# Linear attention and a gated feed-forward in one kernel: groups of 256 tokens in quadrants of the array, with loads and weights gated in order

## The chip, the cores and the metric

One Trainium2 chip, one core of it. The metric is the device time of one execution in microseconds (us), the median over several runs. The profile takes one execution apart; its span is 1.7 to 1.8 us shorter than the time of the same run. PE is the tensor engine, PEld its weight loads, DVE the vector engine (VectorE), ACT the scalar engine (ScalarE), POOL is GpSimd, SP the engine that issues transfers. A run counts as slow when it is over 1.5% above the fastest of the same kernel.

## The reference

Lightning attention (linear attention with a decay per head) and a gated feed-forward on its result, everything in float32:

```python
# q, k, v: [4, 8, 768, 64] (batch, head, token, dim); lam: [8], 0.97 to 0.99
for b in range(nb):                                     # blocks of 64 tokens
    qb, kb, vb = ...
    intra = np.einsum('bhic,bhjc->bhij', qb, kb) * Dmask[None]      # causal lam**(i-j)
    intra = np.einsum('bhij,bhjd->bhid', intra, vb)
    inter = np.einsum('bhid,bhde->bhie', qb * lam_pow[None], kv_state)
    out[:, :, sl] = intra + inter
    kv_state = lam_block * kv_state + np.einsum('bhsd,bhse->bhde', kb * rev_pow, vb)
...
x = out.transpose(0, 2, 1, 3).reshape(3072, 512)
g = x @ w_gate                                          # [512, 1536]
return (g / (1 + np.exp(-g)) * (x @ w_val)) @ w_out     # [1536, 512]
```

Both kernels work in blocks of 128 tokens, which gives the same result.

## The kernel before

Attention goes by pairs of heads: two heads of 64 dimensions fill the 128 rows of the array, q and k are transposed on PE against an identity, and a block of 128 tokens of two pairs is one round, of scores, masks, state reads, products with v and a state update:

```python
for h2 in range(2):                                     # 24 such transfers for one batch
    nc.gpsimd.dma_start(out=q_nat[:, :, h2, :], in_=q_5d[b, hp, h2])   # 96 KB, casts to bf16
    nc.gpsimd.dma_start(out=k_nat[:, :, h2, :], in_=k_5d[b, hp, h2])
    nc.sync.dma_start(out=v_raw[:, :, h2, :], in_=v_5d[b, hp, h2])
...
nc.gpsimd.dma_start(out=wg_sb, in_=moe_w_gate...)       # all gate weights at once, then
nc.gpsimd.dma_start(out=wv_sb, in_=moe_w_val...)        # all value weights, then batch 1
...
nc.tensor.matmul(sp[:, 0, cs], st["kT"][0:64, bs], st["qT"][0:64, bs], start=True, stop=True)
nc.tensor.matmul(sp[:, 1, cs], st["kT"][64:128, bs], st["qT"][64:128, bs], start=True, stop=True)
... # (two halves of the array's rows at a time)
nc.vector.scalar_tensor_tensor(out=st["kv"], in0=st["kv"], scalar=lamblk[hp],
                               in1=up[:, ci, :], op0=ALU.mult, op1=ALU.add)
```

The feed-forward goes by tiles of 512 tokens and by chunks of 128 of the 1536 hidden columns: four gate and four value matmuls of 512 columns per chunk, twelve out matmuls per 128 tokens. Rounds of attention are spread between its chunks.

Of the kernel before, what the change touches and what calls it, by code (L numbers as in the profile page):

```python
# [8 lines left out]
FP32 = mybir.dt.float32  # L10
# [11 lines left out]
def kernel(  # L22
# [11 lines left out]
    nc = tc.nc  # L34

    B, H, S, D = q.shape
# [5 lines left out]
    NTOK = B * S  # L42
    MCHUNKS = DM // 128
    FCHUNKS = DFF // 128
    TT = 512
    NTT = NTOK // TT
    TSUB = 128
    CW = 2
# [3 lines left out]
    xtpool = ctx.enter_context(tc.tile_pool(name="xtpool", bufs=1))  # L52

    qkt_pool = ctx.enter_context(tc.tile_pool(name="qkt", bufs=8))
    nat_pool = ctx.enter_context(tc.tile_pool(name="nat", bufs=8))
    raw_pool = ctx.enter_context(tc.tile_pool(name="raw", bufs=6))
    kv_pool = ctx.enter_context(tc.tile_pool(name="kv", bufs=8))
    ssb_pool = ctx.enter_context(tc.tile_pool(name="ssb", bufs=6))

    hsb_pool = ctx.enter_context(tc.tile_pool(name="hsb", bufs=2))  # L60
    silu_pool = ctx.enter_context(tc.tile_pool(name="silu", bufs=3))
    osb_pool = ctx.enter_context(tc.tile_pool(name="osb", bufs=3))

    apool = ctx.enter_context(tc.tile_pool(name="apool", bufs=3, space=bass.MemoryType.PSUM))
    s_psum = ctx.enter_context(tc.tile_pool(name="s_psum", bufs=1, space=bass.MemoryType.PSUM))
    gate_pool = ctx.enter_context(tc.tile_pool(name="gate_pool", bufs=2, space=bass.MemoryType.PSUM))
    val_pool = ctx.enter_context(tc.tile_pool(name="val_pool", bufs=1, space=bass.MemoryType.PSUM))

    identity = const.tile([128, 128], BF16)
    make_identity(nc, identity)  # L70

    causal01 = const.tile([128, 128], BF16)
    make_upper_triangular(nc, causal01, val=1.0, diag=True)

    iota_free_p1 = const.tile([128, 128], FP32)
    nc.gpsimd.iota(iota_free_p1, pattern=[[1, 128]], base=1, channel_multiplier=0,
                   allow_small_or_imprecise_dtypes=True)
    iota_rev = const.tile([128, 1], FP32)
    nc.gpsimd.iota(iota_rev, pattern=[[0, 1]], base=BLK - 1, channel_multiplier=-1,
                   allow_small_or_imprecise_dtypes=True)  # L80

    lam_bcast = const.tile([128, H], FP32)
    nc.gpsimd.dma_start(out=lam_bcast,
                        in_=bass.AP(tensor=lam.tensor, offset=lam.offset, ap=[[0, 128], [1, H]]))

    q_5d = q.rearrange("b (hp h2) (blk p) d -> b hp h2 p blk d", h2=2, p=128)
    k_5d = k.rearrange("b (hp h2) (blk p) d -> b hp h2 p blk d", h2=2, p=128)
    v_5d = v.rearrange("b (hp h2) (blk p) d -> b hp h2 p blk d", h2=2, p=128)

    loaded = {}  # L90

    def attn_load(b, hp):
        def run():
            q_nat = raw_pool.tile([128, NBLK, 2, D], BF16, name="q_nat", tag="q_nat")
            k_nat = nat_pool.tile([128, NBLK, 2, D], BF16, name="k_nat", tag="k_nat")
            v_raw = nat_pool.tile([128, NBLK, 2, D], FP32, name="v_raw", tag="v_raw", bufs=5)
            for h2 in range(2):
                nc.gpsimd.dma_start(out=q_nat[:, :, h2, :], in_=q_5d[b, hp, h2])  # L98
                nc.gpsimd.dma_start(out=k_nat[:, :, h2, :], in_=k_5d[b, hp, h2])  # L99
                nc.sync.dma_start(out=v_raw[:, :, h2, :], in_=v_5d[b, hp, h2])  # L100
            loaded[(b, hp)] = dict(q_nat=q_nat, k_nat=k_nat, v_raw=v_raw)
        return run

    for hp in range(HP):
        attn_load(0, hp)()

    wg_sb = wpool.tile([128, MCHUNKS, DFF], BF16)
    wv_sb = wpool.tile([128, MCHUNKS, DFF], BF16)
    wo_sb = wpool.tile([128, FCHUNKS, DM], BF16)
    nc.gpsimd.dma_start(out=wg_sb, in_=moe_w_gate.rearrange("(c p) f -> p c f", p=128))  # L110
    nc.gpsimd.dma_start(out=wv_sb, in_=moe_w_val.rearrange("(c p) f -> p c f", p=128))
    for hp in range(HP):
        attn_load(1, hp)()
    nc.gpsimd.dma_start(out=wo_sb, in_=moe_w_out.rearrange("(c p) m -> p c m", p=128))

    ln_lam = const.tile([128, H], FP32)
    nc.scalar.activation(ln_lam, lam_bcast, AF.Ln)

    qscale = []
    revmat = []  # L120
    lamblk = []
    maskp_all = const.tile([128, 2, HP, 128], BF16)
    for hp in range(HP):
        lnp = const.tile([128, 1], FP32, name=f"lnp_{hp}")
        nc.vector.tensor_copy(out=lnp[0:64, :], in_=ln_lam[0:64, 2 * hp:2 * hp + 1])
        nc.vector.tensor_copy(out=lnp[64:128, :], in_=ln_lam[64:128, 2 * hp + 1:2 * hp + 2])

        tmp = raw_pool.tile([128, 128], FP32, name="tmp_c", tag="tmp_c")
        nc.vector.tensor_scalar(out=tmp, in0=iota_free_p1, scalar1=lnp, scalar2=None, op0=ALU.mult)
        qs = const.tile([128, 128], BF16, name=f"qscale_{hp}")  # L130
        nc.scalar.activation(qs, tmp, AF.Exp)
        qscale.append(qs)

        lncols = const.tile([128, 2], FP32, name=f"lncols_{hp}")
        nc.vector.tensor_copy(out=lncols, in_=ln_lam[:, 2 * hp:2 * hp + 2])
        revsmall = const.tile([128, 2], FP32, name=f"revsmall_{hp}")
        nc.vector.tensor_scalar(out=revsmall, in0=lncols, scalar1=iota_rev, scalar2=None, op0=ALU.mult)
        nc.scalar.activation(revsmall, revsmall, AF.Exp)
        rm = const.tile([128, 2, 64], BF16, name=f"revmat_{hp}")
        nc.vector.tensor_copy(out=rm, in_=bap(revsmall, [[1, 2], [0, 64]]))  # L140
        revmat.append(rm)

        for h2 in range(2):
            h = 2 * hp + h2
            invb = raw_pool.tile([128, 1], FP32, name="invb", tag="invb")
            nc.scalar.activation(invb, ln_lam[:, h:h + 1], AF.Exp, scale=-float(BLK))
            nc.vector.tensor_scalar(out=maskp_all[:, h2, hp, :], in0=causal01, scalar1=invb,
                                    scalar2=None, op0=ALU.mult)

        lb = const.tile([128, 1], FP32, name=f"lamblk_{hp}")  # L150
        nc.scalar.activation(lb, lnp, AF.Exp, scale=float(BLK))
        lamblk.append(lb)

    xT = [xtpool.tile([128, NTOK], BF16, name=f"xT_{mc}") for mc in range(MCHUNKS)]

    chain_state = {}

    def attn_prep(b, hp):
        def run():
            ld = loaded.pop((b, hp))  # L160
            q_nat, k_nat = ld["q_nat"], ld["k_nat"]
            v_s = nat_pool.tile([128, NBLK, 2, D], BF16, name="v_s", tag="v_s")
            nc.vector.tensor_tensor(out=v_s, in0=ld["v_raw"],  # L163
                                    in1=bap(revmat[hp], [[0, NBLK], [64, 2], [1, 64]]),
                                    op=ALU.mult)

            qT = qkt_pool.tile([128, S], BF16, name="qT", tag="qT")
            kT = qkt_pool.tile([128, S], BF16, name="kT", tag="kT")
            tpq = apool.tile([128, NBLK, 128], BF16, name="tpq", tag="a")
            for blk in range(NBLK):  # L170
                nc.tensor.transpose(tpq[:, blk, :], q_nat[:, blk, :, :], identity)  # L171
            nc.vector.tensor_tensor(out=qT.rearrange("p (blk s) -> p blk s", blk=NBLK),
                                    in0=tpq, in1=bap(qscale[hp], [[0, NBLK], [1, 128]]),
                                    op=ALU.mult)
            tpk = apool.tile([128, NBLK, 128], BF16, name="tpk", tag="a")
            for blk in range(NBLK):
                nc.tensor.transpose(tpk[:, blk, :], k_nat[:, blk, :, :], identity)  # L177
            nc.scalar.copy(out=kT.rearrange("p (blk s) -> p blk s", blk=NBLK), in_=tpk)  # L178

            kv = kv_pool.tile([128, D], BF16, name="kv", tag="kv")  # L180
            nc.vector.memset(kv, 0.0)

            chain_state[(b, hp)] = dict(qT=qT, kT=kT, k_nat=k_nat, v_s=v_s, kv=kv)
        return run

    wave_state = {}

    def attn_block_front(b, hps, blk):
        def run():
            bs = slice(blk * BLK, (blk + 1) * BLK)  # L190
            n_c = len(hps)
            sp = s_psum.tile([128, 2, 512], FP32, name="sp", tag="sp")
# [86 lines left out]
    def interleave(a_items, f_items):  # L279
        if not a_items:  # L280
            return list(f_items)
# [55 lines left out]
    pos = 0  # L337
# [49 lines left out]
```

## Time and profile before

| | before |
|---|---|
| time | 298.54 us (298.12 to 298.69, 3 runs) |
| span of the profiled run | 295.9 us |
| PE busy | 256.3 us (87%) |
| before the first gate matmul | 52.6 us |

The profile page cuts the span into 40 slices of 7.4 us; a digit is the busy share in tenths. The lines on which the prediction rests stand in it. Two more of the same page are wanted later: the clock granted to PE in tenths of full speed, and what the transfers moved in each slice.

```profile
PEclk9999999999999999999999999999999999999999
GB/s 153 169 169 189 209 189 157 172 182 194 168 128 115 37 39 35 73 124 35 2 35 38 34 5 35 39 0 35 38 15 23 35 35 8 29 37 38 35 72 106
```

The first seven slices move at most 209 GB/s. The clock digits of these slices mislead: the trace's record of the clock begins only at 56.05 us, and time without a record is counted as full. Until then PE ran at half clock: transposes start 0.107 us apart up to 29 us and the first wide matmuls 0.43 us apart near 53 us, where 0.056 and 0.216 us are the rule later. From 56.05 us on the clock is full until PE ends.

### The profile page before, as it was taken

To read this page: it belongs to the slowest core of one execution; us is meant where nothing else is said; L and a number is where in the kernel's file an instruction comes from. 1 tells how busy PE (TensorE), PEld (TensorE's weight loads), DVE (VectorE), ACT (ScalarE), POOL (GpSimd) and SP (SyncE) were. 2 spreads that over 40 slices of the span, in tenths; PEclk is the share of its full clock that TensorE was granted. 3 is DMA by queue.
4 is the path that set the end of the run, shared out by engine and by line. 5 is a ranking of instruction groups with operands and counts; after the bars stand their busy time and mean duration, and the time that the engine had idled before them with its cause. 6 is when DMAs were issued, how large, how long until landed. Compare 5 with 4: busy or idle time off the path is not lost.

```text
span 295.9 us, 4660 instructions
## 1 busy us (share of the span) xinstructions
PE 256.3 (87%) x1824; PEld 119.3 (40%) x1824; DVE 127.2 (43%) x296; ACT 96.6 (33%) x232; POOL 57.0 (19%) x78
## 2 busy tenths in 40 slices
PE   0233614999999999999999999999999999999995
PEld 0122302446444444464444445544444444444442
DVE  1662525477654533934453444345344433222200
ACT  3411201536342422263333224524322332222321
POOL 9765015453156000840000000000000000000000
PEclk9999999999999999999999999999999999999999
DMA  9999999999999110990001000100100000001012
GB/s 153 169 169 189 209 189 157 172 182 194 168 128 115 37 39 35 73 124 35 2 35 38 34 5 35 39 0 35 38 15 23 35 35 8 29 37 38 35 72 106
DMA packets 81383, 23.90 MB, mean 81 GB/s; under 512 B 75729, under 2 KB 77265, under 8 KB 81361
## 3 DMA queue, kind: packets, MB, share of 16 engines
q0 software_dynamic: 52816, 11.02, 41.8%
q1 hardware_dynamic: 28544, 12.59, 19.9%
q8 instruction: 14, 0.23, 0.3%
q14 instruction: 9, 0.07, 0.1%
HBM read 28.32 MB, written 6.29 MB: 117 GB/s over the span
## 4 chain that ended last, share of the span: by engine, by line
PE 82%; DMA 13%; POOL 1%; DVE 1%; issue 1%; ACT 0%; SPq 0%; ACTq 0%; DVEq 0%; POOLq 0%
PE gp L255 24%; PE vp L261 22%; PE ffn_op L272 22%; DMA v_raw<-in_v_dram 8%; PE op L225 3%; DMA q_nat<-in_q_dram 3%; PE sp L196 3%; PE op L217 3%; DMA k_nat<-in_k_dram 2%; PE tpq L171 2%; PE tpk L177 1%; PE up L232 1%; DVE ssb L204 1%; PE sp L198 1%; DVE v_s L163 0%
## 5 line engine op out<-in xcount | busy, mean ns | idle before, releaser
L263 DVE TENSOR_TENSOR h_sb<-sil,vp 128x512 bf16<-128x512 bf16 x72 | 49.5, 687 | 83.7 <-PE vp L261 81.1
L272 PE MATMUL ffn_op<-wo_sb,h_sb 128*128 128x512 bf16 x288 | 65.4, 379 | 0.2
L258 ACT ACTIVATE sil<-gp 128x512 bf16<-128x512 f32 x72 | 43.0, 598 | 60.6 <-PE gp L255 60.2
L204 DVE TENSOR_TENSOR ssb<-sp,maskp_all 128x512 bf16<-128x512 f32 x48 | 33.0, 686 | 32.5 <-PE sp L198 32.5
L261 PEld LDWEIGHTS <-wv_sb 128*128 128x128 bf16 x288 | 28.0, 98 | 35.0 <-issue 3.1
L272 PEld LDWEIGHTS <-h_sb 128*128 128x128 bf16 x288 | 27.7, 98 | 31.9 <-issue 0.2
L99 POOL DMA_DIRECT2D k_nat<-in_k_dram x32 | 26.4, 830 | 52.6 <-PE up L234 24.6
L275 ACT COPY osb<-ffn_op 128x512 f32<-128x512 f32 x24 | 14.1, 586 | 62.7 <-PE ffn_op L272 62.7
L255 PEld LDWEIGHTS <-wg_sb 128*128 128x128 bf16 x288 | 23.5, 98 | 22.9 <-issue 0.3
L98 POOL DMA_DIRECT2D q_nat<-in_q_dram x32 | 26.6, 833 | 18.8 <-DMA wg_sb<-in_moe_w_gate_dram 7.3
L255 PE MATMUL gp<-xT_285,wg_sb 128*128 128x512 bf16 x72 | 28.1, 390 | 0.0
L255 PE MATMUL gp<-xT_286,wg_sb 128*128 128x512 bf16 x72 | 27.6, 383 | 0.0
L255 PE MATMUL gp<-xT_287,wg_sb 128*128 128x512 bf16 x72 | 27.6, 383 | 0.0
L255 PE MATMUL gp<-xT_288,wg_sb 128*128 128x512 bf16 x72 | 27.6, 383 | 0.0
L261 PE MATMUL vp<-xT_285,wv_sb 128*128 128x512 bf16 x72 | 27.5, 382 | 0.0
L261 PE MATMUL vp<-xT_286,wv_sb 128*128 128x512 bf16 x72 | 27.5, 382 | 0.0
L261 PE MATMUL vp<-xT_287,wv_sb 128*128 128x512 bf16 x72 | 27.3, 379 | 0.0
L261 PE MATMUL vp<-xT_288,wv_sb 128*128 128x512 bf16 x72 | 27.3, 379 | 0.0
L171 PE MATMUL tpq<-identity,q_nat 128*128 128x128 bf16 x96 | 9.2, 240 | 20.1 <-DMA q_nat<-in_q_dram 20.1
L225 PE MATMUL op<-ssb,v_s 128*64 128x128 bf16 x96 | 15.0, 241 | 12.4 <-DVE ssb L204 12.4
L178 ACT COPY kT<-tpk 128x768 bf16<-128x768 bf16 x16 | 12.8, 799 | 23.2 <-PE tpk L177 23.0
L198 PE MATMUL sp<-qT,kT 64*128 64x128 bf16 x96 | 16.4, 237 | 0.0
(90 smaller groups left out, 264.2 us busy)
## 6 DMA issues: line engine op xcount, KB each, us to landing
v_raw<-in_v_dram SPq DMA_DIRECT2D x32, 192.0 KB, 9.4
out_dram<-osb SPq DMA_DIRECT2D x24, 256.0 KB, 2.0
q_nat<-in_q_dram POOLq DMA_DIRECT2D x32, 96.0 KB, 9.5
k_nat<-in_k_dram POOLq DMA_DIRECT2D x32, 96.0 KB, 9.7
wg_sb<-in_moe_w_gate_dram POOLq DMA_DIRECT2D x1, 1536.0 KB, 17.1
wv_sb<-in_moe_w_val_dram POOLq DMA_DIRECT2D x1, 1536.0 KB, 24.5
wo_sb<-in_moe_w_out_dram POOLq DMA_DIRECT2D x1, 1536.0 KB, 18.5
lam_bcast<-in_lam_dram POOLq DMA_DIRECT2D x1, 4.0 KB, 4.1
```

Of the source, the lines that this page charges most:

```text
L98: nc.gpsimd.dma_start(out=q_nat[:, :, h2, :], in_=q_5d[b, hp, h2])
L99: nc.gpsimd.dma_start(out=k_nat[:, :, h2, :], in_=k_5d[b, hp, h2])
L171: nc.tensor.transpose(tpq[:, blk, :], q_nat[:, blk, :, :], identity)
L198: nc.tensor.matmul(sp[:, 1, cs], st["kT"][64:128, bs], st["qT"][64:128, bs], start=True, stop=True)
L204: nc.vector.tensor_tensor(out=ssb, in0=sp_ap, in1=mp_ap, op=ALU.mult)
L225: nc.tensor.matmul(op[0:64, :], st["v_s"][:, blk, 0, :], ssb[:, 0, ci, :], start=False, stop=True)
L255: nc.tensor.matmul(gp, wg_sb[:, mc, fs], xT[mc][:, ts], start=(mc == 0), stop=(mc == MCHUNKS - 1))
L258: nc.scalar.activation(sil, gp, AF.Silu)
L261: nc.tensor.matmul(vp, wv_sb[:, mc, fs], xT[mc][:, ts], start=(mc == 0), stop=(mc == MCHUNKS - 1))
L263: nc.vector.tensor_tensor(out=h_sb[:, fc, :], in0=sil, in1=vp, op=ALU.mult)
L272: nc.tensor.matmul(op, h_sb[:, fc, sub * TSUB:(sub + 1) * TSUB], wo_sb[:, fc, :], start=(fc == 0), stop=(fc == FCHUNKS - 1))
L275: nc.scalar.copy(out=osb, in_=op)
```

## The change

The intent: a group is now 256 tokens of all eight heads. The tokens go on partitions in their natural order in pairs (a partition holds two neighbouring tokens, so a piece in memory is 512 B), the array is used as four quadrants of 64x64, and the second tile of 512 tokens is worked as two half tiles, so that its feed-forward can start when only the first of its two groups is attended. From the fifth group on the DMA transposes q and k. Loads and weight pieces are issued in a hand-made order: GpSimd copies one column of a tile that has to have landed (a gate), so that what it issues afterwards can't take bandwidth from what is needed first. A load can be held back too: with `load_group(g, True)` VectorE first writes one column of the tile, and the transfer goes out only when VectorE has come to that place in its list. The diff, cut to its core:

```diff
-    for hp in range(HP):
-        attn_load(0, hp)()
-    nc.gpsimd.dma_start(out=wg_sb, in_=moe_w_gate.rearrange("(c p) f -> p c f", p=128))
-    nc.gpsimd.dma_start(out=wv_sb, in_=moe_w_val.rearrange("(c p) f -> p c f", p=128))
+    def w_piece(c0, c1):
+        cs = slice(c0 * 128, c1 * 128)
+        nc.gpsimd.dma_start(out=wg_sb[:, :, cs], in_=wg_d[:, :, cs])
+        nc.gpsimd.dma_start(out=wv_sb[:, :, cs], in_=wv_d[:, :, cs])
...
+        for c in range(2):                    # scores(g)
+            for hi in range(2):
+                for s in range(2):
+                    for b2 in range(2):
+                        for h2 in range(2):
+                            hp = 2 * c + hi
+                            dp = slice(h2 * 64, h2 * 64 + 64)
+                            n = (hi * 2 + s) * BLK
+                            nc.tensor.matmul(                              # L276
+                                sp[(c, h2)][b2 * M:b2 * M + M, n:n + BLK],
+                                tt[dp, 0, s, hp, b2 * M:b2 * M + M],
+                                tt[dp, 1, :, hp, b2 * M:b2 * M + M],
+                                start=True, stop=True, skip_group_check=True)
...
+            nc.scalar.copy(out=xt[:, :, 2 * (g % 2) + r].rearrange("p h (m s) -> p h s m", s=2),
+                           in_=op[r].rearrange("p (h s m) -> p h s m", h=HP, s=2))   # L356
...
+    def gate(what, g):
+        nc.gpsimd.tensor_copy(out=gate_t, in_=st[(what, g)][:, 0, 0:1])    # L423
...
+    warm_up(13)                               # matmuls on zeros, for the clock
+    cast_qk(0)
+    v_scale(0, nc.gpsimd)
+    w_piece(0, 1)
+    w_piece(1, 2)
+    pe_transpose(0)
...
+    v_scale(1, nc.gpsimd)
+    w_piece(2, 4)
+    w_piece(4, 6)
+    w_piece(6, 8)
+    w_piece(8, 10)
...
+    segment(0, 2, 0, 4)                       # chunks 2 to 11 of the first tile
+    at(5, load_group, 2, True)
+    at(5, gate, "kraw", 2)
+    at(5, w_piece, 10, 12)
+    at(5, v_scale, 2, nc.gpsimd)
+    at(8, load_group, 3, True)
+    at(8, gate, "kraw", 3)
+    for c in range(0, FC, 3):
+        at(8, wo_piece, c, c + 3)
+    at(8, v_scale, 3, nc.gpsimd)
+    at(9, cast_qk, 2)
+    at(10, pe_transpose, 2)
+    at(11, ahead, 2)
+    at(11, core, 2)
+    at = base(len(steps))
+    segment(1, 0, 0, 2)                       # first half of the second tile
+    at(0, cast_qk, 3)
...
```

`at(5, f)` puts f behind chunk 5. `ahead` is the state update and the scores of a group, `core` its state reads, products with v and the copy of the result (L356) into `xt`, the feed-forward's operand. The state update's sums are added on GpSimd and cast into `kvz`, which the state reads need.

## The prediction

> **What bounds the kernel now.** I read the busy shares first, then the 40 slices, then the chain that ended last, then the waits of the tensor engine (PE), and last a table of three stretches and a close look at one microsecond of matmuls. The page:
>
> ```profile
> span 295.9 us, 4660 instructions
> PE 256.3 (87%) x1824; PEld 119.3 (40%) x1824; DVE 127.2 (43%) x296; ACT 96.6 (33%) x232; POOL 57.0 (19%) x78
> PE   0233614999999999999999999999999999999995
> DMA  9999999999999110990001000100100000001012
> DMA packets 81383, 23.90 MB, mean 81 GB/s; under 512 B 75729, under 2 KB 77265, under 8 KB 81361
> PE 82%; DMA 13%; POOL 1%; DVE 1%; issue 1%; ACT 0%; SPq 0%; ACTq 0%; DVEq 0%; POOLq 0%
> PE gp L255 24%; PE vp L261 22%; PE ffn_op L272 22%; DMA v_raw<-in_v_dram 8%; PE op L225 3%; DMA q_nat<-in_q_dram 3%; PE sp L196 3%; PE op L217 3%; DMA k_nat<-in_k_dram 2%; PE tpq L171 2%; PE tpk L177 1%; PE up L232 1%; DVE ssb L204 1%; PE sp L198 1%; DVE v_s L163 0%
> ```
>
> Two regimes: for seven slices PE is mostly idle while the DMA is full, then PE is full to the end. The chain says the same: 13% of the span is transfers, 82% is PE, and three feed-forward matmul lines (gate, value, out) make 68%. No other engine is above 43%. The stretches (columns: PE, weight loads, VectorE, ScalarE, GpSimd, clock, DMA share, GB/s) and PE's own waits give the boundary:
>
> ```profile
> 0.00:52.60 52.60, 16.84 (x172) 10.23 (x172) 23.51 (x74) 11.79 (x41) 26.48 (x41) 1.00 1.46 176
> 52.60:292.30 239.70, 239.42 (x1656) 109.04 (x1652) 103.73 (x223) 84.18 (x190) 30.54 (x37) 1.00 0.44 60
> 292.30:295.90 3.60, 0.00 (x0) 0.00 (x0) 0.00 (x0) 0.59 (x1) 0.00 (x0) 0.87 0.19 73
> ...
> PE tpq L171 <- DMA q_nat<-in_q_dram: 20.1, 4, 10.9
> PE op L225 <- DVE ssb L204: 12.4, 6, 5.5
> ```
>
> So 52.6 us pass before the first gate matmul, 239.7 us are solid PE work, 3.6 us are the last copy and store. In the first stretch PE waits 20.1 us for q and 12.4 us for masked scores; the chain there is one transfer of v, issued at 23.7 us and landed 22.86 us later.
>
> How much of the solid stretch is needed? In the chain, 60 out matmuls take 12.96 us, so 0.216 us each. The feed-forward part has 2 x 288 + 288 = 864 of them: 186.6 us. The rest, 53.1 us, is attention inside the stretch. One round of it, between two feed-forward chunks:
>
> ```profile
> 140.96 0.38 PE L261 MATMUL vp<-xT_288,wv_sb 128*128 128x512 bf16 x1
> 141.27 0.24 PE L217 MATMUL op<-qT,kv 64*64 64x128 bf16 x1
> 141.27 0.24 PE L219 MATMUL op<-qT,kv 64*64 64x128 bf16 x1
> 141.35 0.22 PE L217 MATMUL op<-qT,kv 64*64 64x128 bf16 x1
> 141.35 0.22 PE L219 MATMUL op<-qT,kv 64*64 64x128 bf16 x1
> ...
> 142.01 0.39 PE L255 MATMUL gp<-xT_285,wg_sb 128*128 128x512 bf16 x1
> ```
>
> The reader should see that the matmuls go in pairs that start together, one pair each 0.08 us, and that one round (two head pairs, one block of 128 tokens) costs 142.01 - 141.17 = 0.84 us. 40 of the 48 rounds lie in this stretch (80 of 96 scores on each line): 33.6 us; 144 PE transposes at about 0.055 us are 8 us; some 11.5 us are changes between shapes, a slow clock at the start (0.43 us per wide matmul near 53 us) and single waits.
>
> [...]
>
> **The change part by part.** It is a rewrite with a hand-made order. Counted in the order of PE's instructions: 464 matmuls of 512 columns and 224 of 256 for gate and value, 288 out matmuls, 384 scores, 384 value products, 320 state updates, 80 state reads, 64 transposes, 24 warm-up matmuls. Six terms make the time.
>
> A, the start of full-width feed-forward. Before, a tile of 512 tokens of one batch has to wait for four blocks of all heads, whose loads are 24 transfers of 256 B pieces, with batch 1 and the weights among them. After, a group is 256 tokens of all heads, three loads of 512 KB in 512 B pieces; only two groups (3.1 MB) and two weight chunks (1 MB) are needed for the first work, and weights are released behind v by GpSimd. At an estimated 250 GB/s (above the 176 of the small pieces) plus some 3 us of issue and landing (outputs land in 2.0 us), k and q of group 0 are there at 7 to 8 us. VectorE is at constants and masks until about 10 to 11 us; then cast 1, transposes and their decay product 2 (two of 0.69), scores 0.7, four masks 4 x 0.69 = 2.8, products 1, two ScalarE evictions 1.2: about 19.5 us. Group 1 repeats transposes, scores and masks up to 25.5, its products and evictions reach 27, with two half chunks inside; two more half chunks make 28 us. Warm-up matmuls fill idle time and cost nothing.
>
> B, feed-forward left from there: 464 x 0.216 + 224 x 0.108 + 288 x 0.216 = 186.6 us, as before, since 256 columns take half (estimate); 4 half chunks (32 x 0.108 = 3.5) are already done: 183.1 us.
>
> C, attention left: ten groups. With four quadrants a round of four takes the 0.08 us of a pair: scores 8 x 0.08, value products 8 x 0.08, updates 8 x 0.04 (pairs of 64 columns at 0.03 to 0.04), state reads 8 x 0.06, five changes of shape at 0.1: 2.6 us. Before, the same 256 tokens took four rounds, 3.4, plus 16 transposes, 0.9, plus changes. Transposes move to the DMA for groups 4 to 11; groups 2 and 3 keep theirs, 1 us each. 10 x 2.65 + 2 = 28.5 us.
>
> D, stalls: 3 us. The last weight chunk pair waits for k of group 2, which is issued only after chunk 5: k needs about 4 us, then 1 MB of weights beside 1 MB of q and v about 8; the four chunks 6 to 9 give 6.9 us plus the lag. And each DMA transpose has only some 8 us between its casts and its scores.
>
> E, the tail: the last eviction is halved over two engines and two queues: 2.5 us instead of 3.6. F, the time runs 298.5 - 295.9 = 2.6 us over the span, as now.
>
> Sum: 28 + 183.1 + 28.5 + 3 + 2.5 + 2.6 = 247.7; I say 247.5 us, 17% less. Of the 51 us gained, some 24 come from the start, 25 from the solid stretch (239.7 to 214.6), 1 from the tail. ScalarE (about 100 us busy) and VectorE (about 105: 58 x 0.69 + 28 x 0.42 products, 48 x 0.69 masks, casts) stay below half and do not bound.
>
> **The rivals.** First, quadrants do not overlap four ways: if rounds go two by two, or PE is fed its many small instructions too slowly, C grows by 1.3 to 2 us per group, to 261 to 267 us. For it: a group is 208 instructions, far more than lie in any burst of this trace. Against: in the 0.84 us round 32 instructions pass, and in its densest 0.17 us eight matmuls start. Second, the DMA transpose takes the place of PE's: if one takes 12 us under load instead of the 8 allowed, eight groups stall by 4 us each: 280 us. Against: steady load is 12.6 MB over 190 us, far below what the DMA moves. Third, the opening stays bound by transfers: tile 0 needs all of gate and value weights (6.3 MB) plus groups 0 and 1 by about 43 us; at 176 GB/s that is 54 us and the result is 258 us; at 300 or more nothing stalls and A shrinks by 3, to 243. Fourth, the eight-bank ring of PSUM makes PE wait for evictions after each group: 1 us each, 258 us. Against: the other engines are half idle.
>
> **Range and chances.** The terms B, E and F are firm to 2 us; A to 4, C to 8, D to 8, mostly upward. So 238 to 260 holds eight times in ten. For no gain over 2%, two of the rivals would have to come true in full, or the transposes to take 15 us: faster 0.96, same 0.02, slower 0.02.
>
> **What would show it.** A: full-width gate matmuls begin near 28 us and PE's digits are 9 from the fifth slice on. B: 0.216 us per wide matmul. C: four matmuls of 64x64 start within 0.03 us, and score lines repeat every 0.08. D: waits of PE for a DMA of value weights once, none for transposed q and k. I would be wrong by the first rival if a group took over 4 us of PE, by the second if scores waited for the transposed tile in each group, by the third if gate matmuls wait for weights several times before 45 us.

No run then on record had shown four quadrants at work at once; that a round of four takes the 0.08 us of a pair, on which C rests, was assumed. The 250 GB/s in A are an estimate which the page before bears out only roughly: the packets of one queue (12.59 MB in 28544) took 19.9% of 16 engines' 295.9 us, 214 GB/s, the smaller ones of another (11.02 MB in 52816) 41.8%, 89 GB/s. The 4 and 8 us in D, estimates too, fit the 250: 0.52 MB are 2.1 us, with the 2.0 us in which an output landed 4.1; 2.1 MB are 8.4 us. The steady load of the second rival is 66 GB/s (12.6 MB over 190 us) against 176 moved in the loading stretch.

## The result and the profile after

| | before | after |
|---|---|---|
| time, median | 298.62 us (298.12 to 299.5, 4 runs) | 268.48 us (266.47 to 270.84, 4 runs, one of them slow) |
| ratio of fast runs | | 0.8971, 95% interval 0.8934 to 0.9009 |
| span of the profiled run | 295.9 us | 264.8 us |
| mean granted clock of the runs, as recorded | 0.998 to 1.0 | 0.93 to 0.948 |

A ratio is the mean time of one kernel's fast runs over the mean of the other's fast runs of the same rounds, so not quite the ratio of the medians quoted. The change is 10.3% faster: well beyond noise, and some 21 us above the 247.5 us predicted. The clocks of the two can't be compared: the record begins at 56.05 us before and at 6.17 us after, and what lies ahead of it is counted as full. With half clock up to there, the profiled runs come to about 0.90 before and 0.94 after (my estimate).

The page of the kernel after, in the lines that answer to those of before:

```profile
span 264.8 us, 5375 instructions
PE 232.8 (88%) x2232; PEld 125.5 (47%) x2232; DVE 104.5 (39%) x194; ACT 102.0 (39%) x185; POOL 75.8 (29%) x114
PE   8476699185988998979999899998999998999994
PEclk9775999868699999999999999999999999999999
GB/s 138 336 123 181 100 1 155 272 234 139 0 29 346 226 77 187 214 228 131 272 87 185 175 45 286 70 214 186 40 118 3 40 42 0 40 42 41 40 76 83
PE 74%; DMA 10%; ACT 7%; DVE 4%; issue 2%; POOL 2%; ACTq 0%; SPq 0%; DVEq 0%; POOLq 0%
```

Here the slices are 6.6 us. PE is at work almost from the start, as meant, but its digit falls to 1 in the eighth slice, in the middle of the feed-forward, and the clock digits are 8, 6, 8, 6 around there. The transfers moved 1 GB/s in the sixth slice, just before. So something was waited for at 48 us that the DMA had time for at 35 us. The chain has 10% of transfers and 7% of ACT left. (The clock of the first slice is again one without a record: the 13 warm-up matmuls there start 0.43 us apart until 5.9 us.)

The stretches (columns: start and end, length, then busy time and count of PE, weight loads, DVE, ACT and GpSimd, the clock, the DMA's share and GB/s) divide it at the first full-width matmul, at the first out matmul and at the last one:

```profile
0.00:33.55 33.55, 22.32 (x288) 13.45 (x289) 17.51 (x44) 15.63 (x31) 18.48 (x36) 0.80 0.98 173
33.55:81.15 47.60, 35.99 (x386) 21.06 (x384) 18.57 (x45) 17.35 (x32) 16.46 (x26) 0.86 0.58 128
81.15:261.30 180.15, 174.51 (x1562) 91.03 (x1559) 68.04 (x104) 68.65 (x124) 40.87 (x52) 1.00 0.43 124
261.30:264.80 3.50, 0.00 (x0) 0.00 (x0) 0.42 (x1) 0.34 (x1) 0.00 (x0) 1.00 0.21 75
```

The long third stretch is nearly solid: 174.5 of 180.2 us busy at full clock. The second is not: 36.0 of 47.6 us, at a clock of 0.86. PE's waits (total us, times, longest) say for what:

```profile
PE bank L378 <- ACT xt L356: 7.8, 6, 2.4
PE bank L378 <- DMA wg_sb<-in_moe_w_gate_dram: 5.8, 1, 5.8
PE bank L237 <- ACT qk L221: 4.6, 2, 2.9
PE bank L332 <- POOL kvz L320: 2.5, 2, 1.5
```

And the timeline of the moment (start, length, engine, line, operation, in brackets the wait before it and what ended it):

```profile
46.85 0.19 POOL L423 COPY gate_t<-kraw 128x1 f32<-128x1 f32 x1 [24.33 <-DMA kraw<-in_k_dram]
47.30 0.75 POOL L178 DMA_DIRECT2D wg_sb<-in_moe_w_gate_dram  x1 [0.27 <-issue]
...
53.35 1.89 PE L378 MATMUL bank<-xt,wg_sb 128*128 128x512 bf16 x4 [5.82 <-DMA wg_sb<-in_moe_w_gate_dram]
55.87 1.76 PE L385 MATMUL bank<-xt,wv_sb 128*128 128x512 bf16 x4 [0.64 <-DMA wv_sb<-in_moe_w_val_dram]
```

GpSimd stands 24.33 us at the gate, until the k of the third group (number 2) lands; that load was itself held back until 41.47 us. Only then, at 47.30, does it issue the weights of chunks 10 and 11; PE has finished chunk 9 at 47.5 and idles to 53.35. The four matmuls then take 1.89 us in place of 1.03: while PE idled its clock was halved. The trace records the half clock from 50.5 to 57.4 us, and once more from 64.2 to 71.0 (the expectations below give these times 0.2 to 0.3 us too late), after a stretch of 3.8 us in which PE worked 1.68 us between waits for `kvz` and `xt`. The opening has two such periods, 9.6 to 16.4 and 19.8 to 26.7, besides the half clock before the record. All four are 6.83 us long; in the trials there are also 3.41 (the last one) and 10.24 (the early weights, the dummy matmuls).

Half clock began at 50.5, 3.0 us after PE had stopped at 47.5 (PE was busy for 0.03 us in between), and ended at 57.4, 4.0 us after PE had started again. What rule sets its start and its length is not shown.

### The profile page after: what moved, and what is told of

Its sections match the earlier page's. It is cut to its first block, busy times and chain, and to the rows that moved or that the text cites. A ratio compares the mean times of both kernels' runs of the same rounds, so it can differ in the third digit from the quotient of the medians.

```text
span 264.8 us, 5375 instructions
## 1 busy us (share of the span) xinstructions
PE 232.8 (88%) x2232; PEld 125.5 (47%) x2232; DVE 104.5 (39%) x194; ACT 102.0 (39%) x185; POOL 75.8 (29%) x114
## 4 chain that ended last, share of the span: by engine, by line
PE 74%; DMA 10%; ACT 7%; DVE 4%; issue 2%; POOL 2%; ACTq 0%; SPq 0%; DVEq 0%; POOLq 0%
PE bank L395 23%; PE bank L385 22%; PE bank L378 22%; DMA kraw<-in_k_dram 5%; ACT xt L356 3%; DMA wv_sb<-in_moe_w_val_dram 3%; PE bank L347 2%; DMA qkt<-qk 2%; DVE ssb L283 2%; PE bank L237 1%; PE bank L332 1%; PE bank L276 1%; ACT kvz L320 1%; DVE h L388 1%; ACT qk L221 1%
## 5 line engine op out<-in xcount | busy, mean ns | idle before, releaser
L388 DVE TENSOR_TENSOR h<-sil,bank 128x512 bf16<-128x512 bf16 (+1 forms) x86 | 51.2, 600 | 125.9 <-PE bank L385 97.4
L378 PE MATMUL bank<-xt,wg_sb 128*128 128x512 bf16 (+1 forms) x344 | 79.5, 355 | 14.4 <-ACT xt L356 7.8
L385 PE MATMUL bank<-xt,wv_sb 128*128 128x512 bf16 (+1 forms) x344 | 78.6, 352 | 0.8 <-DMA wv_sb<-in_moe_w_val_dram 0.6
L382 ACT ACTIVATE sil<-bank 128x512 bf16<-128x512 f32 (+1 forms) x86 | 45.0, 529 | 66.0 <-PE bank L378 61.1
L395 PE MATMUL bank<-wo_sb,h 128*128 128x512 bf16 x288 | 65.6, 379 | 0.0
L395 PEld LDWEIGHTS <-h 128*128 128x128 bf16 x288 | 28.2, 98 | 32.8 <-issue 0.2
L402 ACT COPY osb<-bank 128x512 f32<-128x512 f32 (+1 forms) x24 | 13.8, 576 | 62.4 <-PE bank L395 60.4
L283 DVE TENSOR_TENSOR ssb<-bank,mask 128x512 bf16<-128x512 f32 x48 | 31.4, 684 | 11.9 <-PE bank L276 11.7
L188 POOL TENSOR_TENSOR v_s<-v,rev 128x1024 bf16<-128x1024 f32 x12 | 24.7, 2059 | 15.9 <-DMA v<-in_v_dram 7.9
L356 ACT CAST xt<-bank 128x512 bf16<-128x512 f32 x24 | 15.9, 733 | 13.6 <-PE bank L347 13.6
L320 POOL CAST kvz<-kvf 64x256 bf16<-64x256 f32 x32 | 12.6, 394 | 1.7
L212 DVE TENSOR_TENSOR qk<-qraw,qd 128x1024 bf16<-128x1024 f32 x8 | 10.3, 1288 | 0.0
```

The lines of the kernel that those rows point to most:

```text
L188: eng.tensor_tensor(out=st[("vs", g)][:, h0:h1], in0=st[("v", g)][:, h0:h1].rearrange("p h (s d) -> p h s d", s=2), in1=bap(rev, [[2, h1 - ...
L283: nc.vector.tensor_tensor(out=ssb[:, h2, 2 * c:2 * c + 2].rearrange("p a s n -> p (a s n)"), in0=sp[(c, h2)], in1=mask[:, h2, 2 * c:2 * c ...
L320: e_copy(out=kvz[b][(i + 1) % 2 if r else 2][dp, :, h2, :], in_=kvf[b][dp])
L356: nc.scalar.copy(out=xt[:, :, 2 * (g % 2) + r].rearrange("p h (m s) -> p h s m", s=2), in_=op[r].rearrange("p (h s m) -> p h s m", h=HP, s=2))
L378: nc.tensor.matmul(gp[:, 0:N], wg_sb[:, mc, fs], xt[:, mc, b0:b1].rearrange("p b n -> p (b n)"), start=(mc == 0), stop=(mc == MC - 1))
L382: nc.scalar.activation(sil[:, 0:N], gp[:, 0:N], AF.Silu)
```

## The experiments

All edits are against the kernel after, unless said otherwise. Where I give where the first out matmul started, compare with 81.15 us after. The expectations count groups from 0: their group 2, or "the second group" beside "the third", is the third group of the text.

### The last weight pieces released early

My theory after reading the trace: the early part is short by a chain of waits that starts with the gated weights.

```diff
     w_piece(8, 10)
+    w_piece(10, 12)
...
-    at(5, w_piece, 10, 12)
```

> Only the release of the last gate and value weights (chunks 10 and 11) moves: out of the gate behind k of group 2, into the opening behind chunks 8 and 9, where the trace of the changed kernel shows the DMA at rest from 30 to 43 us. Theory (the gate made PE wait): the waits of 5.8 and 0.6 us on these weights go, with them the half clock from 50.8 to 57.6 us (8 wide matmuls at 0.43 in place of 0.216, 1.7 us), so about 8 us less, near 260. Part may come back if group 2, whose v lands at about 50 us, is then what PE waits for. Rival (the opening is short of bandwidth, the weights would come late anyway): same waits within 2 us, time unchanged. Second rival (the wait only hides attention work of group 2): the wait moves to the scores of group 2, gain under 2 us.

Measured: 264.6 us (263.71 to 264.9, 4 fast runs), ratio to before 0.8878 [0.8861, 0.8895], so some 3 to 4 us faster than the kernel after, and the first out matmul at 77.39. No wait for weights is left. In their place PE waits once at the state reads, shown here with GpSimd's timeline of that moment:

```profile
PE bank L332 <- POOL kvz L320: 5.4, 1, 5.4
```

```profile
50.25 1.90 POOL L188 TENSOR_TENSOR v_s<-v,rev 128x1024 bf16<-128x1024 f32 x1 [2.70 <-DMA v<-in_v_dram]
52.10 0.18 POOL L423 COPY gate_t<-kraw 128x1 f32<-128x1 f32 x1
52.28 3.12 POOL L182 DMA_DIRECT2D wo_sb<-in_moe_w_out_dram  x4
55.43 1.92 POOL L188 TENSOR_TENSOR v_s<-v,rev 128x1024 bf16<-128x1024 f32 x1
57.27 0.41 POOL L315 COPY kvf<-ups 128x256 f32<-128x256 f32 x1
```

The state update of the third group (57.27) stands behind the gate of the fourth (52.10), four issues of out weights (3.12 us) and the scaling of the fourth group's v (1.92 us). PE, which no longer waits for weights, comes to it earlier and meets this list. (In the kernel after the same v landed 10.9 us after its issue, and GpSimd scaled it at 59.42.) The wait moved, and with it the half clock: 10.24 us of it a little later, from about the same cause. (The recorded clock of 0.954 over a span of 262.0 us leaves 24.1 us at half, the opening's included.)

### The load of the third group freed too

```diff
-    at(5, load_group, 2, True)
-    at(5, gate, "kraw", 2)
+    at(5, load_group, 2)
```

(on top of the previous trial)

> As the first, and the loads of group 2 are not gated any more: they go out behind group 1. Theory: k, q and v of group 2 land before 35 us, so its casts and scaling are long done when PE needs them; weights land some 5 us later than now but still before their use. Besides the 8 us of the first run the waits around 61 to 65 us may shrink: 257 to 261. Rival (the gates protect the opening: 1.5 MB more in front of the weights delays full-width work): first full-width matmul moves from 33.5 to 37 or later, and the run is slower than the first one by 3 us or more.

Measured: 263.92 us (263.09 to 264.93), ratio 0.8854 [0.8827, 0.888]: the same as the previous trial within the intervals. The wait at the state reads is still 4.8 us. Landing earlier helps nothing while GpSimd's list holds the state update back.

### GpSimd's list in another order, gates kept

This isolates that list. On top of the early weights, what belongs to the fourth group is moved behind the third's state update:

```diff
-    at(8, gate, "kraw", 3)
-    for c in range(0, FC, 3):
-        at(8, wo_piece, c, c + 3)
-    at(8, v_scale, 3, nc.gpsimd)
     at(9, cast_qk, 2)
     at(10, pe_transpose, 2)
     at(11, ahead, 2)
     at(11, core, 2)
+    at(11, gate, "kraw", 3)
+    for c in range(0, FC, 3):
+        at(11, wo_piece, c, c + 3)
+    at(11, v_scale, 3, nc.gpsimd)
```

> The run with the last weight pieces released in the opening, and in addition GpSimd's list for the third group (the gate on its k, the out-weight pieces, the scaling of its v) moved behind the state update of the second group; all gates on loads are kept. Main theory (GpSimd is in order, and the work of a later group stood ahead of the state update that the tensor engine waited for): the wait on kvz at the readout of the key sums falls from 5.4 us in the run with early weights to under 1.5 us, and the time from 264.6 to 259 to 261 us. Rival (that wait was only the last of several; the loads themselves are late): the wait reappears on v, on the out weights or on the k of the third group, and the time stays at 263 to 266 us.

Measured: 259.09 us (255.86 to 260.85, 4 runs, one slow), ratio 0.8654 [0.8609, 0.87], 5.5 us by the medians under the trial with early weights alone (6.7 us by the ratios of the fast runs). The first out matmul starts at 70.53, the last ends at 250.59. GpSimd's timeline:

```profile
53.23 0.40 POOL L315 COPY kvf<-ups 128x256 f32<-128x256 f32 x1 [1.10 <-ACT ups L309]
53.69 0.84 POOL L320 CAST kvz<-kvf 64x256 bf16<-64x256 f32 x2
...
57.56 0.19 POOL L423 COPY gate_t<-kraw 128x1 f32<-128x1 f32 x1
57.69 2.35 POOL L182 DMA_DIRECT2D wo_sb<-in_moe_w_out_dram  x3
```

The update now waits for its own input alone and comes 4 us sooner; the wait of 5.4 us is one of 1.4 and one of 1.0, and the trace has no half clock between the opening and the tail (a recorded clock of 0.979 over 254.1 us leaves 10.7 us at half, for 24.1 in the trial with early weights). Main theory confirmed: with the same gates and the same transfers, only the order in the list was changed.

### All loads and weights of the early part freed

```diff
     w_piece(8, 10)
+    w_piece(10, 12)
...
-    at(5, load_group, 2, True)
-    at(5, gate, "kraw", 2)
-    at(5, w_piece, 10, 12)
+    at(5, load_group, 2)
...
-    at(8, load_group, 3, True)
-    at(8, gate, "kraw", 3)
+    at(8, load_group, 3)
```

> As the second run, and the loads of group 3 and the out weights are not gated either; nothing in GpSimd's order waits for a late load any more. Theory (GpSimd works in order, and its state update of group 2 stood behind the gate on k of group 3, four out-weight issues of 3.1 us and the scaling of v of group 3): the wait of PE on the state of group 2 falls from 4.8 us to under 1.5 us, no weight waits, the half clock between 58 and 65 us goes: 6 to 8 us under the second run, near 257. Rival (the state update is slow by itself): the wait stays at 4 to 5 us. Second rival (1.5 MB more ahead of the weights starves the first tile): gate or value matmuls wait for weights, the time stays at 262 or more.

Measured: 256.4 us (255.58 to 261.37, the last slow), ratio 0.8591 [0.8564, 0.8618], 12 us under the kernel after. The first out matmul starts at 71.23, the last ends at 251.33: between the two 180.1 us, as after. So all of the gain lies before 81.15, and it is what the waits for weights and `kvz` and the half clock cost there together. As the previous trial gets nearly as far with the gates of the loads in place, it is the order in GpSimd's list and the late weights that cost, and hardly the gating of k, q and v.

### The clock alone: dummy matmuls in the gap

```diff
     at(9, cast_qk, 2)
+    at(9, warm_up, 26)
```

> 26 dummy matmuls of 512 columns (5.6 us at 0.216) in front of chunk 10 of the first tile, so that PE is busy while it waits for the gated weights. It parts the wait from the clock. Theory (the half clock follows the idle of PE): the weights come no earlier, but the clock stays full to 58 us; chunks 10 and 11 take 1.7 instead of 4.1 us including the wait between them; gain 1.5 to 2.5 us, near 266. Rival (the half clock has another cause[...]): clock still 0.5 somewhere in 50 to 58 us, gain under 0.5 us or a loss.

Measured: 267.6 us (266.71 to 272.91, the last slow), ratio 0.8966 [0.8939, 0.8993]: no gain. In its profile (of the slow run) the clock did stay full in the gap, from 27.0 to 64.6 us, which speaks for PE's idling as the cause of the half clock. But waits of 1.7 and 1.5 us for the weights were left behind the dummies, the later wait at the state reads was 5.9 us, and 10.24 us of half clock began in it (0.956 over 271.2 us leaves 23.9 us at half, the opening's included). A miss for the clock as a cause by itself: its cure at this one place gained nothing in the fast runs. Why is not shown: in the slow run, the only one with a profile, GpSimd stood until 64.4 us for the v of the fourth group, 5 us longer than in the kernel after.

### Scores by quadrant

Does the overlap of the four quadrants rest on the order of the instructions, as I had assumed?

```diff
-            for hi in range(2):
-                for s in range(2):
-                    for b2 in range(2):
-                        for h2 in range(2):
+            for b2 in range(2):
+                for h2 in range(2):
+                    for hi in range(2):
+                        for s in range(2):
```

> Same 384 score matmuls of 64x64, but with the loop over the quadrants outermost, so that four in a row use the same quadrant. Theory (four quadrants run side by side): 32 matmuls take 1.3 to 1.8 us in place of the 0.54 to 0.6 of the changed kernel, 10 groups of them on the path: 8 to 12 us slower, near 278. Rival (PE is bound by the number of instructions, not by their place): 0.55 us as now and the same time within 1%.

Measured: 269.72 us (266.79 to 271.24, one slow), ratio 0.9014 [0.8957, 0.9071], against 0.8971: the same time within the intervals, and a miss. The 32 scores of a group, first in the kernel after, then in this trial:

```profile
97.99 0.62 PE L276 MATMUL bank<-qkt 64*64 64x128 bf16 x32
```

```profile
98.07 0.69 PE L276 MATMUL bank<-qkt 64*64 64x128 bf16 x32
```

Though four matmuls of one quadrant now follow each other in the instruction order, the burst grew from 0.62 to 0.69 us only, and in the last four groups it even went from 0.70 to 0.68.

### Two quadrants in place of four

All scores read rows 0 to 63, so that only two quadrants work.

```diff
-                            dp = slice(h2 * 64, h2 * 64 + 64)
+                            dp = slice(0, 64)
```

> The changed kernel, but all score matmuls read rows 0 to 63, so that they use two quadrants of the array instead of four; the result is wrong on purpose. Theory that the quadrants are what makes attention cheap: the burst of 32 score matmuls takes about 0.9 us in place of 0.44 us, 0.45 us more per half group, about 4 to 5 us more in all, so about 273 us. Rival (the burst is bound by issue or by something other than the array): the same 0.44 us and 267 to 269 us.

Measured: 273.56 us (268.33 to 278.97, two of four slow), ratio 0.9059 [0.9005, 0.9114]. The burst:

```profile
102.78 1.06 PE L276 MATMUL bank<-qkt 64*64 64x128 bf16 x32
```

1.06 in place of 0.62 us: 0.44 us more, as expected (though a burst is all scores of a group, not of half a group), and pairs of starts where there were fours. The time moved by less than I expected, 0.9% of 298 us or some 2.6 us by the fast runs, and the intervals of the two ratios just touch. From the first to the last out matmul it is 181.8 us against 180.1, while the bursts of the eight groups in it are 3.2 us longer in sum; part fell into waits, as PE's idle time there went from 5.6 to 4.2 us. That four quadrants work at once is shown; its worth in time only roughly.

### The DMA transposes undone

```diff
-    at(10, cast_scaled, 4)
+    at(10, cast_qk, 4)
+    at(1, pe_transpose, 4)
...
-                at(1 + j, cast_scaled, g)
+                at(1 + j, cast_qk, g)
+                at(3 + j, pe_transpose, g)
```

(and so for groups 5 and 6, each transposed on PE two or three chunks behind its cast)

> The changed kernel with the DMA transposes undone: groups 4 to 11 are transposed on PE like groups 0 to 3, two chunks ahead of their use. Theory (a transposed group costs PE 0.89 us and its DMA form nothing but one wait of 0.9 us): 8 x 0.89 - 0.9 = 6 us more, near 274.5. Rival (the DMA transposes delay the loads behind them on the same queue, and PE transposes keep everything flowing): same or faster.

Measured: 274.89 us (272.59 to 277.0, one slow), ratio 0.9194 [0.9148, 0.9241], against 0.8971: 6.6 us more. Eight groups at 0.89 us of PE for transposes would be 7.1 us. This part of the change does what it was meant to.

### The second group of a tile attended one chunk earlier

```diff
-            at(11, attend, 2 * t + 3)
+            at(10, attend, 2 * t + 3)
```

> The changed kernel with one edit in the steady part: the attention of the second group of a tile is put one chunk earlier, so that one chunk of the old tile stands between its evictions and the next tile's first gate matmul. Theory (PE waits there for two ScalarE evictions, 0.72, 0.72 and 1.40 us): these three waits go, 2.5 to 3 us less, near 265.5 against 268.5. Rival (ScalarE is behind anyway): waits move to the next bank, gain under 1 us.

Measured: 267.28 us (265.59 to 271.19, one slow), ratio 0.8946 [0.8902, 0.8989], not apart from 0.8971. In the profile the waits for `xt` fell from 7.8 to 5.0 us and the part between first and last out matmul from 180.1 to 177.1 us, as meant; but in that run the wait for weights was 7.5 and that for `kvz` 4.9 us. The edit does not touch the early part, so this is not the same from run to run; in the profiled run it hid the 3 us.

### More warm-up in the opening

On top of the trial with all loads freed: 26 warm-up matmuls for 13, 10 for 7, and 8 and 7 more around the second group's transposes.

```diff
-    warm_up(13)
+    warm_up(26)
...
-    warm_up(7)
+    warm_up(10)
...
+    warm_up(8)
     pe_transpose(1)
+    warm_up(7)
```

> As the run before it in this batch, with more dummy matmuls in the opening: 26 in place of 13 at the start, 10 in place of 7, and 8 and 7 more around the transposes of group 1. Theory (the half clock from 9.8 to 16.6 and from 20.0 to 26.9 us in the changed kernel comes from idle PE): the clock stays full in the opening, the first full-width matmul moves 2 to 3 us earlier, time 2 to 3 us under e6. Rival (the opening is bound by casts, masks and evictions on other engines): start moves by under 1 us; dummies that overrun may even cost 1 us.

Measured: 258.34 us (254.26 to 260.01, two of four counted slow), ratio 0.8583 [0.8513, 0.8654], against 0.8591. Inconclusive for the time: the profiled run had a clock of 0.991 and a span of 252.6 us, the others clocks of 0.972 to 0.98. In that run the opening did get shorter, as the theory said: the wait for `xt` ends at 30.74 us for 33.06 without the warm-up, and the first full-width matmul starts at 32.70 for 35.02.

### All remedies together

On top of the trial with all loads freed: the group attended one chunk earlier; the groups 2 and 3 cast, transposed and attended some chunks earlier; and `xt` laid out by halves, since a strided write of one half (L356) was held to touch the other half's tile and blocked its matmuls.

```diff
-        st[("xt", t)] = xt_pool.tile([128, MC, B, BLK], BF16, name="xt", tag="xt")
+        st[("xt", t)] = xt_pool.tile([128, B, MC, BLK], BF16, name="xt", tag="xt")
...
-    at(9, cast_qk, 2)
-    at(10, pe_transpose, 2)
-    at(11, ahead, 2)
-    at(11, core, 2)
+    at(6, cast_qk, 2)
+    at(7, pe_transpose, 2)
+    at(8, ahead, 2)
+    at(10, core, 2)
+    at(9, cast_qk, 3)
+    at(11, pe_transpose, 3)
...
-    at(0, cast_qk, 3)
-    at(3, pe_transpose, 3)
-    at(4, ahead, 3)
+    at(0, ahead, 3)
-    at(7, core, 3)
+    at(5, core, 3)
```

> The run without gates on the loads of the second and third group, and in addition: the second group of each tile is attended one chunk earlier, the transposed operand tile is laid out with the heads' halves apart so that a write of one half no longer blocks a matmul of the other, and the casts, transposes and cores of the second and third group are placed a few chunks earlier in the first tile. Main theory (what is left over 240 us is waits for the evacuation of attention and a slow opening): the xt waits of 7.8 us fall under 3 us and the time from 256.4 to 248 to 251 us. Rival (the waits only move, as in the trial with dummy matmuls, because the same scalar and vector engine chains then come later than the tensor engine): 254 to 257 us.

Measured: 249.81 us (249.15 to 251.64, 6 fast runs), ratio 0.8395 [0.8363, 0.8427]; correct. Its stretches, divided at the same instructions as those of the kernel after:

```profile
0.00:34.39 34.39, 20.80 (x286) 12.88 (x289) 20.11 (x44) 15.63 (x31) 22.69 (x40) 0.80 1.14 236
34.39:67.39 33.00, 31.17 (x386) 19.44 (x384) 17.96 (x39) 17.00 (x32) 12.58 (x20) 1.00 0.64 101
67.39:244.65 177.26, 173.76 (x1549) 90.84 (x1559) 69.95 (x104) 68.46 (x123) 40.05 (x52) 1.00 0.45 128
```

The second stretch holds the same 386 matmuls in 33.00 us for 47.60, at clock 1.00 for 0.86: 14.6 us. The third is 2.9 us shorter. Of the waits for `xt` one of 2.4 us is left, in the opening. The first stretch is no shorter. How the last 6.6 us against the trial with all loads freed divide between the three edits was not tried apart, but for the 3 us that the earlier attendance alone took from the steady part.

### The same with more warm-up

> The same with more warm-up matmuls in the opening (26, 10, 8 and 7). Theory that the half clock of the opening costs what the first full-width matmul comes late: it starts about 2 us earlier and the time is 1 to 3 us under the version without. Rival: the clock granted later is lower in turn, and the time is the same within its scatter of some 2 us.

(the edit of the earlier warm-up trial on top of the last one)

Measured: 249.36 us (249.24 to 250.01, 4 fast runs), ratio 0.8369 [0.8348, 0.8389]. The intervals overlap: the same time, with a clock of 0.993. The half clock of the opening is down to one period of 3.41 us (0.993 over 247.7 us leaves 3.5 us at half), but that one falls on the last four half chunks before full width, from 30.4 us on. They are released by the wait for `xt`, first without the warm-up, then with it:

```profile
32.65 0.60 PE L378 MATMUL bank<-xt,wg_sb 128*128 128x256 bf16 x4 [2.41 <-ACT xt L356]
```

```profile
31.15 1.01 PE L378 MATMUL bank<-xt,wg_sb 128*128 128x256 bf16 x4 [2.53 <-ACT xt L356]
```

The wait ends 1.5 us earlier, but the half chunks then take 3.05 us for 1.74, and the first full-width matmul starts at 34.20 for 34.39. The rival holds: the half clock moved. It also shows that PE's clock has a share in the length of the opening, 1.5 us here and 2.3 us in the earlier warm-up trial.

## Why the prediction was right or wrong

The gain was foreseen in kind and the time was not: 268.48 us lies outside 238 to 260. By the prediction's terms, on the profiled run (264.8 us of span, 266.47 of time; the median is 2 us above):

| term | predicted | measured | how |
|---|---|---|---|
| A, start of full width | 28 | 33.55 | first matmul of 512 columns on all of a tile |
| B, feed-forward left | 183.1 | 183.1 | kept, as 512 columns took 0.216 us and 256 took 0.109 |
| C, attention of ten groups | 28.5 | 23.2 | what remains of 33.55 to 261.23 without B and D |
| D, stalls | 3 | 21.4 | PE's waits from 33.55 on (16.8) and what the half clock added (4.6) |
| E, tail | 2.5 | 3.5 | last matmul to the end |
| F, time over span | 2.6 | 1.7 | 266.47 - 264.8 |

**D is the step that failed**, and it outweighs all the rest: "D, stalls: 3 us. The last weight chunk pair waits for k of group 2, which is issued only after chunk 5". The place was right and the size was not. The prediction's own figures give more: 4 + 8 us for k and the weights against 6.9 us for chunks 6 to 9 leave 5.1 us, and the trace has 5.8 (k from its issue at 41.47 to the gate 5.4, the weights from theirs at 47.30 to their first matmul 6). I wrote 3 for this and all other stalls together. What followed it I did not see at all: GpSimd's list, in which the next state update stood behind another group's gate, out-weight issues and v (1.5 us in the kernel after, 5.4 once PE came sooner), the waits for `xt` behind it, and the half clock that each of these gaps brings on (4.6 us: 1.8 on the eight matmuls from 53.35 on, 2.8 on the half chunks from 64.4 on). Together that is 16.1 us before the first out matmul. The trials show it from the other side: the early weights take 4 us, the order of GpSimd's list another 5.5, all remedies of the early stretch 14.6. Some 5.3 us of D, of which 2.8 wait for `xt`, lie in the steady part, where one edit took 3.

**A, 5.5 us late.** k landed at 8.4 us and its transposes ended at 11.4, as predicted or sooner, and the first group's scores started at 12.33; GpSimd scaled v in 1.90 us. The time went later. On ScalarE the second group's chain carries what the sum left out: a table load (1.28 us) and four copies of the state (0.82 each pair), of which the last pairs stand ahead of the copies to `xt` that PE waits 2.4 us for. And "Warm-up matmuls fill idle time and cost nothing" did not keep the clock: PE ran at half clock from 9.6 to 16.4 and 19.8 to 26.7 us all the same, in the opening's own chain. More of them brought the wait for `xt` forward by 1.5 and 2.3 us (the two warm-up trials), so the clock accounts for some 2 us of A. ScalarE's and VectorE's chain is what I take to set the rest; that is read from the trace and was not tried.

**B and the order of magnitude of C were right, C to the good side.** A group costs PE about 2.0 us (updates 0.28, scores 0.44 from first start to last start, state reads 0.55, products 0.47, the rest changes), for 2.65 predicted; with 0.9 for each of two transposes on PE that is 21.8 of the 23.2 left over. What made it short: I had taken the round of four to take 0.08 us like the pair before, and it takes 0.056. The trial with two quadrants shows that four start at once because of the quadrants; but its pairs too start every 0.056 us, so the shorter round is not their doing, and why the pair before took 0.08 stays open. **E and F**: halving the last eviction did not shorten the tail (3.5 us for 3.6 before), and F had set the median time against the span of the profiled run, while every run that lists both has 1.7 to 1.8.

**The rivals.** The first (quadrants don't overlap) is refuted. The second (DMA transposes late) too: they land 4.3 us after issue, scores waited for one once (0.9 us), and undoing them costs 6.6 us. The third (opening bound by transfers) came true in another form: not bandwidth, since up to 346 GB/s were moved and the DMA lay idle from 30 to 41 us, but the order of issue. That "gate matmuls wait for weights several times before 45 us" did not happen; once, at 47.5, was enough. The fourth (PSUM ring) is refuted as to size: one gate matmul waited 0.6 us at 100.2 for `ups`, the copy that frees its bank, nothing like 1 us for each group.

**The ranges.** D was given 8 us of play "mostly upward" and missed by 18. The kernel with all remedies runs 249.81 us, near the predicted 247.5, and its terms can be checked with the same B and C: 34.4 + 183.1 + 23.2 + 4.3 (its waits from there on) + 3.6 + 1.7 = 250.3, for 249.94 of the profiled run. That it comes near is partly luck: A is 6.4 us longer than in the sum and C 5.3 shorter.

## What to carry to other kernels

When transfers are gated to protect bandwidth, take the time at which each gate opens, add issue and landing, and compare it with the instant its consumer is due: the number for the stall is that difference, not a lump sum, and an idle DMA just before a wait for data means that the gate was set too late (here 1 GB/s from 33.1 to 39.7 us, and a wait of 5.8 us from 47.5). An engine that both issues transfers and computes in order, as GpSimd does here, must have the work that others wait for ahead of the work of later groups (its list in another order took 5.5 us off). A long stall of the tensor engine was paid twice here, since its clock was halved (5.8 us of waiting brought 1.8 us more), so count the waits and the half-clock periods together and expect one cured wait to uncover the next.

## What else the runs showed

- With the scores ordered quadrant by quadrant the burst of 32 took 0.69 us, for 0.62 interleaved. Four in a row in one quadrant, one per 0.056 us, eight times over, would need about 1.3 us if each waited with its start for the one before (my estimate from the trace's round). The overlap across quadrants did not depend on the order of the source here; whether the compiled program keeps that order was not checked.
- The half-clock periods past the opening, at 4.6 us, were a fifth of the 21.4 us of stalls of a kernel that was busy 88% of its span.
- A DMA transpose of a group (16 tiles of 128x128, 512 KB) landed 4.3 us after issue (the median of eight, 3.7 to 5.3), 0.27 us a tile; a transfer of a single tile is in no trace here.
- The time of a kernel with stalls scattered with its clock: the fast runs of the kernel after took 266.47 to 268.6 us at recorded clocks of 0.948 to 0.94 and its slow one 270.84 at 0.93, while the kernel before, whose PE works without long waits once its clock is full, kept within 298.12 to 299.5.
